# An expert stage with two units, not one, on the early routing: seven pairs and five singles follow in turn

## The chip, the core and the metric

The kernel runs on one core of a Trainium2 chip. The metric is the time of one execution on the device in microseconds, lower is better. PE is the matrix engine (TensorE), DVE is VectorE, ACT is ScalarE, POOL is GpSimd, SP is the engine whose queue issues most transfers.

## The reference

Attention over pooled queries, then a gated feed-forward block, then a mixture of eight experts of which each token takes two. All 1152 tokens (two batches of 576) go through all three. The change touches the last part alone:

```python
logits = x @ w_gate
noise_scale = np.log1p(np.exp(x @ w_noise))
noisy_logits = logits + noise_scale * noise
top2 = np.argpartition(-noisy_logits, 2, axis=1)[:, :2]
...
for e in range(E):
    for k in range(2):
        mask = top2[:, k] == e
        ...
        h = np.maximum(x[mask] @ w1[e], 0.0)
        out[mask] += top2_w[mask, k, None] * (h @ w2[e])
```

x is 1152 x 512, w1 is 8 x 512 x 1024, w2 is 8 x 1024 x 512, all float32.

## The kernel before

Every float32 product is made as three products of split operands (high and low parts), so each weight that is loaded is first split: a cast by ACT (w_hi, L993) and a subtraction by DVE (w_lo, L997).

**Blocks and units.** The tokens of each expert fill blocks of 128 slots, up to nine per expert. A unit is one set of expert weights (4 MB, eight loads of 512 KB) used on two blocks (a pair) or on one (a single). SEQ (L926) is the order of the units: the first, u0, then eight pairs and five singles in the order P S P P S P S P P S P S P. Which expert and which blocks the r-th pair or single has is computed on the chip (r_blocks, L869, and r_index, L911). Units past NPS pairs and NSS singles are guarded by the flag `more` (L1180); it is true when the routing needs more pairs or singles than these.

**Early routing.** The routing of the first 512 tokens (tiles 0 to 3) is computed during the feed-forward stage, in small steps that a hand-written plan (T_A, L1190) puts between its products. r_first (L824) counts the choices of these tokens, finds the most chosen expert (`ea`, `ef`), and marks its first block and, where there are 256 or more choices, its second (`sel0`). e_preload (L938) loads that expert's weights, e_gather0 (L958) gathers its tokens' rows. r_parity (L850) and `selx` take these blocks out of what r_blocks hands to the later units.

**The opening.** From L1333 to L1419 the order of u0 is written out by hand, since each engine works its instructions in program order: quarters of the first weight (up, L1054; each ends in an evacuation by ACT and DVE, up_evac, L1063), eight groups of the second (down, L1081), the splits of weights, and between them the routing of the other five tiles: gB is the top-2 chain and the slot assignment (with block sums on POOL at L747 and L749, which the product at L754 reads), gW the routing weights, gC the block lists (r_blocks), gH the one-hot tables, then r_table and r_index. Only behind these can the expert of u1 be read (`ti`, L903), its weights be loaded (wload, L987) and its rows be gathered (gather_x, L1005), transposed (x_trans, L1046) and used.

**The later units.** units (L1131) runs u1 to u13. A unit has eight pieces: four up, four down. Weights are split five pieces ahead; the load of a unit goes into one of two sets of buffers and is issued as the unit two before it is split. At piece 0 of unit u the result of u-1 is finished (finish, L1112): DVE scales it, adds the partial rows `pr`, and POOL scatters each block to the output in HBM (L1122). At piece 2, gather_o (L1012) fetches the partial rows of u from the output; it comes after the scatters of u-1, as both may name the same tokens. At piece 5 the next unit's rows are transposed, and the rows of the one after it gathered. Two PSUM banks hold up products (`ph`), so the fourth quarter of a pair needs the second one's bank to be evacuated; the evacuation by DVE stands behind finish of the unit before.

Of the kernel before, what the change touches and what calls it, by code (L numbers as in the profile page):

```python
# [21 lines left out]
def fused_kernel(ctx, tc, q, k, v, w_gate, w_val, w_out, rms_g,  # L22
# [539 lines left out]
    NPS, NSS = 8, 5  # L562
# [10 lines left out]
    def r_iotas():  # L573
# [35 lines left out]
        rtile("sel0", [P, 2])  # L609
# [214 lines left out]
    def r_first():  # L824
# [11 lines left out]
        dve.tensor_copy(rtile("ea", [P, 1], I32), kx[:, 0:1])  # L836
        dve.tensor_copy(rtile("ef", [P, 1]), kx[:, 0:1])
        yield
        d9, full = rtile("d9", [P, 1]), rtile("full", [P, 2])
        dve.scalar_tensor_tensor(d9, R["ef"], -float(NT), R["ip"], op0=ALU.mult, op1=ALU.add)  # L840
        dve.tensor_scalar(full[:, 0:1], k8[:, 0:1], float(2 * P * NE), None, op0=ALU.is_ge)
        yield
        sel, sx = R["sel0"], rtile("selx", [P, 1])
        dve.tensor_scalar(sel[:, 0:1], d9, 0.0, None, op0=ALU.is_equal)
        dve.tensor_scalar(sel[:, 1:2], d9, 1.0, full[:, 0:1], op0=ALU.is_equal, op1=ALU.mult)
        yield
        dve.tensor_tensor(sx, sel[:, 0:1], sel[:, 1:2], op=ALU.add)
        yield

    def r_parity():  # L850

        full, hot = R["full"], rtile("hot", [P, 1])
        dve.tensor_scalar(full[:, 1:2], full[:, 0:1], -1.0, 1.0, op0=ALU.mult, op1=ALU.add)
        dve.tensor_scalar(hot, R["er"], R["ef"], full[:, 1:2], op0=ALU.is_equal, op1=ALU.mult)
        yield
        dve.tensor_tensor(R["ev"], R["ev"], hot, op=ALU.not_equal)
        yield

    def r_index0():
        tab = rtile("tab0", [P, P])  # L860
        act.copy(tab[0:NCOL], PB["t"][0:NCOL, 0:P])
        yield 1
        pi = pst.tile([P, 512], F32, name="pi0", tag="T")
        pe.matmul(pi[:, 0:2], tab[0:NCOL], R["sel0"][0:NCOL], start=True, stop=True)
        yield 1
        dve.tensor_scalar(rtile("idx0", [P, 2], I32), pi[:, 0:2], float(BIG), None, op0=ALU.add)
        dve.tensor_scalar(rtile("gidx0", [P, 2], I32), pi[:, 0:2], float(BIG), QF - 1.0, op0=ALU.add, op1=ALU.min)
# [43 lines left out]
    def r_index(pl):  # L911
# [14 lines left out]
    SEQ = [None] + [(True, 0), (False, 0), (True, 1), (True, 2), (False, 1), (True, 3), (False, 2), (True, 4),  # L926
                    (True, 5), (False, 3), (True, 6), (False, 4), (True, 7)]
# [3 lines left out]
    def nblk(u):  # L931
        return 2 if u == 0 or SEQ[u][0] else 1

# [47 lines left out]
    def experts():  # L981
# [5 lines left out]
        def wload(u, i):  # L987
            if i == 0:
                c = ucol(u, 0)
                REG[u] = sp.value_load(R["ti"][0:1, c:c + 1], min_val=0, max_val=NE - 1)  # L990
# [13 lines left out]

        def gather_x(u):  # L1005
            XG[u] = mo.tile([P, 2, XW], F32, name="xg", tag="xg", bufs=1)
            for k in range(nblk(u)):
                c = ucol(u, k)
                pool.indirect_dma_start(out=XG[u][:, k], out_offset=None, in_=XD,
                                        in_offset=bass.IndirectOffsetOnAxis(ap=R["gidx"][:, c:c + 1], axis=0))  # L1010

        def gather_o(u):  # L1012
            PR[u] = wps[0].tile([P, 2, DM], F32, name="pr", tag="ws21", bufs=1)
            for k in range(nblk(u)):
                c = ucol(u, k)
                pool.indirect_dma_start(out=PR[u][:, k], out_offset=None, in_=out,
                                        in_offset=bass.IndirectOffsetOnAxis(ap=R["gidx"][:, c:c + 1], axis=0))
# [84 lines left out]
        def weight(u):  # L1102
# [3 lines left out]
            e = R["eb"][:, ucol(u, 0):ucol(u, 0) + 1] if u else R["ef"]  # L1106
# [5 lines left out]
        def finish(u):  # L1112
            n = nblk(u)
            yo = YO[u] = mo.tile([P, 2, DM], F32, name="yo", tag="yo", bufs=1)
            for k in range(n):
# [5 lines left out]
                sx = R["sidx"][:, ucol(u, k):ucol(u, k) + 1] if u else R["idx0"][:, k:k + 1]  # L1121
                pool.indirect_dma_start(out=out, out_offset=bass.IndirectOffsetOnAxis(ap=sx, axis=0),  # L1122
# [212 lines left out]
    gH = r_hot(4, 5, ex["mo"], (("oha", 1), ("ohs", 3)), ())  # L1335
    w_hi(0, 0)
# [7 lines left out]
    r_trans(8, (ps, "gv1", 2))  # L1344
    up(0, 0, 1)
    r_logits(7, 4, 5)
    r_logits(8, 4, 5)
    run(gB, 1)
    w_hi(0, 3)
    up_evac(0, 0)  # L1350
    ex["weight"](0)
    up(0, 1, 0)
    run(gB, 6)
    w_lo(0, 3)
    up(0, 1, 1)
# [91 lines left out]
```

## Time and profile before

| | us |
|---|---|
| three runs | 859.11, 855.58, 857.98 |
| median | 857.98 |
| the profiled execution | 858.63 |
| its span, first to last instruction | 856.8 |
| PE busy in it | 796.3 (93%) |

Lines of the profile name the engine, the line of the kernel, the operation, the tile written and the tiles read. A busy PE is not PE at its peak; PEclk is the granted clock as a share of full speed. Stages by the timeline: attention and feed-forward up to about 537, the expert stage from there to the end.

### The profile page before, as it was taken

The numbers are of one execution on the slowest core, as the hardware profiler recorded it, in microseconds if no ns is written. First come the engines' busy times: TensorE is split into PE (matmuls) and PEld (weight loads), VectorE is DVE, ScalarE is ACT, GpSimd is POOL, SyncE is SP. The second block draws the span as 40 slices with busy tenths as digits, with TensorE's granted clock in tenths as the row PEclk, the third lists the DMA queues.
The fourth block names the chain that finished last, engine by engine and source line by source line (L and its number), as shares of the span: only waits on it lengthen the run. The fifth ranks groups of instructions, "written<-read, shape, count | busy, mean of one in ns | idle before, by whom it ended". The sixth has DMA issues, their size and how long they took to land. (4 is left out here: it accounts for less than half of the span.)

```text
span 856.8 us, 14036 instructions
## 1 busy us (share of the span) xinstructions
PE 796.3 (93%) x5282; PEld 685.7 (80%) x5282; DVE 576.7 (67%) x833; ACT 421.7 (49%) x823; POOL 300.3 (35%) x251
## 2 busy tenths in 40 slices
PE   5999999999898989999999999879989998998993
PEld 4777777777675889999999899859979887998892
DVE  5667667778688755775787454767667666567670
ACT  4665565666565554442333343435635636356550
POOL 8647646649124522221222101013324133132320
PEclk9999999999998989999999999999999999999997
DMA  7344312310133112221331116069997978778410
GB/s 219 88 135 126 101 53 80 101 43 15 42 113 99 50 50 94 103 99 50 99 99 54 50 36 225 26 226 367 375 315 251 303 230 271 239 236 274 144 53 17
DMA packets 72938, 118.82 MB, mean 139 GB/s; under 512 B 7582, under 2 KB 37278, under 8 KB 72864
## 3 DMA queue, kind: packets, MB, share of 16 engines
q1 hardware_dynamic: 67504, 101.55, 37.4%
q0 software_dynamic: 5360, 16.31, 5.5%
q8 instruction: 43, 0.70, 0.4%
q14 instruction: 31, 0.25, 0.1%
HBM read 103.66 MB, written 10.77 MB: 134 GB/s over the span
## 5 line engine op out<-in xcount | busy, mean ns | idle before, releaser
L528 PE MATMUL gv<-XN,ws 128*128 128x256 f32 (+1 forms) x1152 | 168.8, 300 | 4.1 <-ACT sl L536 3.7
L528 PEld LDWEIGHTS gv<-XN,ws 128*128 128x128 f32 x1152 | 160.5, 192 | 10.1 <-ACT sl L536 4.0
L999 DVE TENSOR_TENSOR wz<-raw,wz 128x1024 fp32r<-128x1024 f32 x112 | 133.9, 1221 | 17.7 <-ACT wz L106 17.5
L193 DVE TENSOR_REDUCE Ql<-s 128x1 fp32r<-128x1152 f32 x72 | 97.3, 1355 | 59.0 <-PE s L188 45.1
L1088 PE MATMUL py<-wz,hTT 128*128 128x512 f32 x552 | 134.1, 395 | 0.0
L204 ACT ACTIVATE et<-st 128x288 f32<-128x288 f32 x288 | 103.2, 413 | 54.1 <-PE st L203 49.5
L106 ACT CAST wz<-raw 128x1024 fp32r<-128x1024 f32 x112 | 113.5, 1047 | 10.8 <-PE py L1088 8.0
L1088 PEld LDWEIGHTS py<-wz,hTT 128*128 128x128 f32 x552 | 101.4, 190 | 20.1 <-DVE hTT L971 0.9
L1061 PE MATMUL ph<-xgT,wz 128*128 128x256 f32 x768 | 97.6, 290 | 13.3 <-DVE hTT L1066 12.6
L1061 PEld LDWEIGHTS ph<-xgT,wz 128*128 128x128 f32 x768 | 96.3, 198 | 14.9 <-DVE hTT L1066 13.4
L202 PE MATMUL st<-QH,KT 128*128 128x288 f32 x288 | 91.6, 333 | 5.5 <-ACT et L204 4.0
L398 POOL TENSOR_TENSOR ws<-wm,ws 128x1024 fp32r<-128x1024 f32 x18 | 43.3, 2406 | 151.5 <-ACT ws L397 97.5
L549 PE MATMUL po<-ws,hT 128*128 128x512 f32 x324 | 83.0, 395 | 0.1
L203 PE MATMUL st<-QlT,KT 128*128 128x288 f32 x288 | 82.4, 300 | 0.0
L229 PE MATMUL av<-et,v 128*64 128x288 f32 x576 | 81.9, 420 | 0.0
L202 PEld LDWEIGHTS st<-QH,KT 128*128 128x128 f32 x288 | 55.4, 192 | 20.8 <-ACT et L204 11.6
L217 POOL TENSOR_TENSOR accp<-accp,et 128x576 f32<-128x576 f32 x32 | 48.5, 1517 | 57.1 <-ACT et L204 36.5
L549 PEld LDWEIGHTS po<-ws,hT 128*128 128x128 f32 x324 | 58.4, 188 | 10.7 <-ACT hT L538 0.5
L538 ACT CAST hT<-sl 128x256 fp32r<-128x256 f32 (+1 forms) x48 | 20.8, 434 | 89.4 <-DVE sl L537 89.4
L1122 POOL DMA_INDIRECT out_dram<-yo,sidx x21 | 27.8, 1325 | 90.4 <-DVE yo L1120 52.0
L229 PEld LDWEIGHTS av<-et,v 128*64 128x64 f32 x576 | 37.5, 138 | 26.0 <-issue 5.9
L1065 ACT ACTIVATE hTT<-ph 128x512 fp32r<-128x512 f32 x36 | 21.5, 598 | 72.7 <-PE ph L1061 70.6
(252 smaller groups left out, 1174.3 us busy)
## 6 DMA issues: line engine op xcount, KB each, us to landing
raw<-in_moe_w_dram SPq DMA_DIRECT2D x112, 512.0 KB
wraw<-in_moe_w_gate_dram SPq DMA_DIRECT2D x6, 1024.0 KB
wraw<-in_moe_w_val_dram SPq DMA_DIRECT2D x6, 1024.0 KB
wraw<-in_moe_w_out_dram SPq DMA_DIRECT2D x6, 1024.0 KB
kraw<-in_k_dram SPq DMA_DIRECT2D x16, 288.0 KB
v<-in_v_dram SPq DMA_DIRECT2D x8, 576.0 KB
KT<-KT SPq DMA_DIRECT2D x16, 288.0 KB
Qraw<-in_q_dram SPq DMA_DIRECT2D x16, 256.0 KB
```

The source lines that it names most:

```text
L106: act.copy(o, i)
L193: dve.tensor_reduce(Ql[p % 3][h][:, c, D:D + 1], t[:, :, 0:384], axis=AX.XY, op=ALU.max, negate=True)
L202: pe.matmul(t[:, 0:NG], KT[p, h][:, cs], QhT[p, h][:, n0:n0 + NG], start=True, stop=False)
L203: pe.matmul(t[:, 0:NG], KT2[h][p % NKT[h]][:, cs], QlT[p, h][:, n0:n0 + NG], start=False, stop=True)
L204: act.activation(et[:, h, :], t[:, 0:NG], AF.Exp, scale=SCALE)
L217: eng.tensor_tensor(acc, acc, e, op=ALU.add)
L229: pe.matmul(av[h * D:(h + 1) * D, 0:NG], V[p][:, h, c, :], ET[p, g, c][:, h, :], start=(c == 0), stop=(c == KC - 1))
L528: pe.matmul(t[:, 0:n], w[a][:, d, j * P:(j + 1) * P], XN[hf][b_][:, d, cs], start=(k_ == 0), stop=(k_ == 11))
L549: pe.matmul(pt, HT[f, hf][a][:, j, c0:c0 + P], w[b_][:, j, :], start=(k_ == 0), stop=(k_ == 5))
L999: eng.tensor_tensor(lo, RAW[u % 2][i], hi.bitcast(F32), op=ALU.subtract)
L1061: pe.matmul(o, w[a][:, d, j * P:j * P + P], XT[u][c][:, d], start=z + d == 0, stop=z == 2 and d == 3)
L1088: pe.matmul(PL[u, "y", k], x[c][:, f0 + d, k * P:k * P + P], w[a][:, d], start=i == 4 and z + d == 0, stop=i == 7 and z == 2 and d == 1)
```

## The change

- r_first takes the two most chosen experts of the first 512 tokens. For each, block 0 counts if it has at least 128 choices and block 1 if it has at least 256. `sel0` has four columns, and r_parity and r_index0 follow it (not shown: the parity of an expert is flipped where just one block was taken, and the index tables become four columns wide).
- u0 and u1 are both units of the early routing. u1's weights are loaded and its rows gathered (from the first 512 rows alone) at the start of the opening; u0 is as before.
- NPS is 7, not 8, and the order is now P P, then P S P S P S P S P S P P.
- The opening is written anew: ACT and DVE split weights of u0 earlier, its evacuations stand ahead of routing steps, the transposes of u1 stand between its fifth and sixth piece, and the first splits of u1 follow sooner. The gather and the loads of u2 are issued ahead of u0's last down group.

```diff
@@ -559,7 +559,7 @@
     NCOL = NE * NT
 
     NPA, NSA = 12, NE
-    NPS, NSS = 8, 5
+    NPS, NSS = 7, 5
     NCU = 2 * NPA + NSA
     BIG = B * SQ
     dram = ctx.enter_context(tc.tile_pool(name="xd", bufs=1, space=bass.MemoryType.DRAM))
...
@@ -833,27 +833,33 @@
         yield
         dve.max_index(kx, k8, key)
         yield
-        dve.tensor_copy(rtile("ea", [P, 1], I32), kx[:, 0:1])
-        dve.tensor_copy(rtile("ef", [P, 1]), kx[:, 0:1])
-        yield
-        d9, full = rtile("d9", [P, 1]), rtile("full", [P, 2])
-        dve.scalar_tensor_tensor(d9, R["ef"], -float(NT), R["ip"], op0=ALU.mult, op1=ALU.add)
-        dve.tensor_scalar(full[:, 0:1], k8[:, 0:1], float(2 * P * NE), None, op0=ALU.is_ge)
+        dve.tensor_copy(rtile("ea", [P, 2], I32), kx[:, 0:2])
+        dve.tensor_copy(rtile("ef", [P, 2]), kx[:, 0:2])
+        yield
+
+        d9, full = rtile("d9", [P, 2]), rtile("full", [P, 2, 2])
+        dve.scalar_tensor_tensor(d9, R["ef"], -float(NT), R["ip"].to_broadcast([P, 2]), op0=ALU.mult, op1=ALU.add)
+        for k in range(2):
+            dve.tensor_scalar(full[:, :, k], k8[:, 0:2], float((k + 1) * P * NE), None, op0=ALU.is_ge)
         yield
         sel, sx = R["sel0"], rtile("selx", [P, 1])
-        dve.tensor_scalar(sel[:, 0:1], d9, 0.0, None, op0=ALU.is_equal)
-        dve.tensor_scalar(sel[:, 1:2], d9, 1.0, full[:, 0:1], op0=ALU.is_equal, op1=ALU.mult)
-        yield
-        dve.tensor_tensor(sx, sel[:, 0:1], sel[:, 1:2], op=ALU.add)
+        for z in range(2):
+            for k in range(2):
+                dve.tensor_scalar(sel[:, 2 * z + k:2 * z + k + 1], d9[:, z:z + 1], float(k), full[:, z, k:k + 1],
+                                  op0=ALU.is_equal, op1=ALU.mult)
+        yield
+        dve.tensor_reduce(sx, sel, axis=AX.X, op=ALU.add)
         yield
 
     def r_parity():
 
-        full, hot = R["full"], rtile("hot", [P, 1])
-        dve.tensor_scalar(full[:, 1:2], full[:, 0:1], -1.0, 1.0, op0=ALU.mult, op1=ALU.add)
-        dve.tensor_scalar(hot, R["er"], R["ef"], full[:, 1:2], op0=ALU.is_equal, op1=ALU.mult)
-        yield
-        dve.tensor_tensor(R["ev"], R["ev"], hot, op=ALU.not_equal)
+        full, hot, odd = R["full"], rtile("hot", [P, 2]), rtile("odd", [P, 2])
+        dve.tensor_tensor(odd, full[:, :, 0], full[:, :, 1], op=ALU.subtract)
+        for z in range(2):
+            dve.tensor_scalar(hot[:, z:z + 1], R["er"], R["ef"][:, z:z + 1], odd[:, z:z + 1], op0=ALU.is_equal, op1=ALU.mult)
+        yield
+        for z in range(2):
+            dve.tensor_tensor(R["ev"], R["ev"], hot[:, z:z + 1], op=ALU.not_equal)
         yield
 
     def r_index0():
...
@@ -923,13 +929,13 @@
 
     RAW = []
     REG = {}
-    SEQ = [None] + [(True, 0), (False, 0), (True, 1), (True, 2), (False, 1), (True, 3), (False, 2), (True, 4),
-                    (True, 5), (False, 3), (True, 6), (False, 4), (True, 7)]
+    SEQ = [None, None] + [(True, 0), (False, 0), (True, 1), (False, 1), (True, 2), (False, 2), (True, 3), (False, 3),
+                          (True, 4), (False, 4), (True, 5), (True, 6)]
     NU1 = len(SEQ)
     SEQ += [(True, r) for r in range(NPS, NPA)] + [(False, r) for r in range(NSS, NSA)]
 
     def nblk(u):
-        return 2 if u == 0 or SEQ[u][0] else 1
+        return 2 if u < 2 or SEQ[u][0] else 1
 
     def ucol(u, k):
         pair, r = SEQ[u]
...
@@ -986,8 +992,8 @@
 
         def wload(u, i):
             if i == 0:
-                c = ucol(u, 0)
-                REG[u] = sp.value_load(R["ti"][0:1, c:c + 1], min_val=0, max_val=NE - 1)
+                c = ucol(u, 0) if u > 1 else 1
+                REG[u] = sp.value_load(R["ti" if u > 1 else "ea"][0:1, c:c + 1], min_val=0, max_val=NE - 1)
             e_dma(u, i)
 
         def w_hi(u, i, eng=act):
...
@@ -1002,19 +1008,24 @@
             w_hi(u, i)
             w_lo(u, i)
 
+        def col(u, k, nm):
+            if u < 2:
+                return R[nm + "0"][:, 2 * u + k:2 * u + k + 1]
+            c = ucol(u, k)
+            return R[nm][:, c:c + 1]
+
         def gather_x(u):
             XG[u] = mo.tile([P, 2, XW], F32, name="xg", tag="xg", bufs=1)
             for k in range(nblk(u)):
-                c = ucol(u, k)
-                pool.indirect_dma_start(out=XG[u][:, k], out_offset=None, in_=XD,
-                                        in_offset=bass.IndirectOffsetOnAxis(ap=R["gidx"][:, c:c + 1], axis=0))
+                gi = col(u, k, "gidx")
+                pool.indirect_dma_start(out=XG[u][:, k], out_offset=None, in_=XD if u > 1 else XD[0:QF],
+                                        in_offset=bass.IndirectOffsetOnAxis(ap=gi, axis=0))
 
         def gather_o(u):
             PR[u] = wps[0].tile([P, 2, DM], F32, name="pr", tag="ws21", bufs=1)
             for k in range(nblk(u)):
-                c = ucol(u, k)
                 pool.indirect_dma_start(out=PR[u][:, k], out_offset=None, in_=out,
-                                        in_offset=bass.IndirectOffsetOnAxis(ap=R["gidx"][:, c:c + 1], axis=0))
+                                        in_offset=bass.IndirectOffsetOnAxis(ap=col(u, k, "gidx"), axis=0))
 
         tb = [0]
 
...
@@ -1333,6 +1343,9 @@
     gW = r_weights(4, 5)
     gC = r_blocks()
     gH = r_hot(4, 5, ex["mo"], (("oha", 1), ("ohs", 3)), ())
+    ex["gather_x"](1)
+    for i in range(8):
+        wload(1, i)
     w_hi(0, 0)
     w_lo(0, 0)
     w_hi(0, 1)
...
@@ -1342,78 +1355,72 @@
     up(0, 0, 0)
     w_lo(0, 2)
     r_trans(8, (ps, "gv1", 2))
+    w_hi(0, 3)
+    w_lo(0, 3)
     up(0, 0, 1)
     r_logits(7, 4, 5)
     r_logits(8, 4, 5)
+    up_evac(0, 0)
     run(gB, 1)
-    w_hi(0, 3)
-    up_evac(0, 0)
+    up(0, 1, 0)
+    w_hi(0, 4)
     ex["weight"](0)
-    up(0, 1, 0)
     run(gB, 6)
-    w_lo(0, 3)
+    w_lo(0, 4)
     up(0, 1, 1)
+    up_evac(0, 1)
+    w_hi(0, 5)
+    up(0, 2, 0)
     run(gB, 6)
-    up_evac(0, 1)
-    w_hi(0, 4)
-    up(0, 2, 0)
-    run(gB, 11)
-    w_lo(0, 4)
+    w_lo(0, 5)
     up(0, 2, 1)
     up_evac(0, 2)
-    w_hi(0, 5)
+    run(gB, 11)
+    w_hi(0, 6)
     up(0, 3, 0)
     run(gB, 2)
-    w_hi(0, 6)
+    w_lo(0, 6)
     up(0, 3, 1)
     run(gB, 1)
-    w_lo(0, 5)
     up_evac(0, 3)
-    run(gW, 4)
     down(0, 4, 0)
     run(gB)
+    w_hi(0, 7)
+    down(0, 4, 1)
+    run(gW)
     run(gC, 2)
-    down(0, 4, 1)
+    x_trans(1)
+    down(0, 5, 0)
     run(gH, 1)
-    run(gC, 4)
-    w_lo(0, 6)
-    w_hi(0, 7)
-    down(0, 5, 0)
     run(gC, 2)
-    run(gW)
+    w_lo(0, 7)
+    down(0, 5, 1)
+    run(gC, 2)
     run(gH, 1)
     run(gH, 1)
     run(gH)
-    down(0, 5, 1)
+    w_hi(1, 0)
+    down(0, 6, 0)
     run(gC, 2)
-    wload(1, 0)
-    wload(1, 1)
-    wload(1, 2)
-    wload(1, 3)
+    w_lo(1, 0)
     r_table(4, 5)
-    r_index(ex["mo"])
-    ex["gather_x"](1)
-    w_lo(0, 7)
-    down(0, 6, 0)
     down(0, 6, 1)
     run(gC)
-    for i in range(4, 8):
-        wload(1, i)
-    w_hi(1, 0)
-    w_lo(1, 0)
-    down(0, 7, 0)
-    down(0, 7, 1)
-    w_hi(1, 1)
-    w_lo(1, 1)
-    ex["finish"](0)
-    x_trans(1)
+    r_index(ex["mo"])
     ex["weight"](1)
     ex["gather_x"](2)
-    ex["gather_o"](1)
-    for i in range(2, 5):
-        wsplit(1, i)
     for i in range(8):
         wload(2, i)
+    w_hi(1, 1)
+    down(0, 7, 0)
+    w_lo(1, 1)
+    down(0, 7, 1)
+    w_hi(1, 2)
+    w_lo(1, 2)
+    ex["finish"](0)
+    ex["gather_o"](1)
+    for i in range(3, 5):
+        wsplit(1, i)
     for i in range(5):
         wload(3, i)
     fps.close()
```

## Rows read from the trace of the kernel before

**Rows 1.** The page's costliest groups: busy us, mean ns | idle before.
```profile
L1088 PE MATMUL py<-wz,hTT 128*128 128x512 f32 x552 | 134.1, 395 | 0.0
```

**Rows 2.** Windows: busy us (x count) by engine, PEclk, DMA share, GB/s.
```profile
536.70:576.20 39.50, 31.22 (x204) 26.88 (x204) 27.76 (x86) 15.30 (x28) 5.11 (x7) 0.95 0.34 115
576.20:599.90 23.70, 23.69 (x148) 21.72 (x149) 17.95 (x24) 13.56 (x17) 6.86 (x6) 0.94 1.07 370
599.90:842.20 242.30, 229.58 (x1481) 208.25 (x1479) 160.29 (x201) 124.03 (x157) 70.31 (x56) 0.98 0.73 238
```

**Rows 3.** Waits of PE, 536.7 to 576.2: us, times, longest.
```profile
PE xt L966 <- DMA xg<-XD,gidx: 3.4, 2, 3.0
PE ph L1061 <- DVE hTT L1066: 1.9, 1, 1.9
PE pq L889 <- DVE u L885: 1.6, 1, 1.6
```

**Rows 4.** Timeline of PE: start, us, operation, count [idle before <- releaser].
```profile
550.50 1.89 PE L1061 MATMUL ph<-xt,wz 128*128 128x256 f32 x12 [1.93 <-DVE hTT L1066]
...
552.38 2.91 PE L1061 MATMUL ph<-xt,wz 128*128 128x256 f32 x12
...
576.21 12.48 PE L1061 MATMUL ph<-xgT,wz 128*128 128x256 f32 x96 [0.68 <-ACT xgT L969]
...
639.32 11.47 PE L1061 MATMUL ph<-xgT,wz 128*128 128x256 f32 x96
```

**Rows 5.** Windows right behind a wait of PE.
```profile
550.50:555.30 4.80, 4.80 (x29) 4.71 (x30) 4.66 (x23) 2.57 (x4) 0.99 (x1) 0.64 0.01 2
...
576.20:580.20 4.00, 3.99 (x23) 3.99 (x24) 3.97 (x7) 2.79 (x3) 0.99 (x1) 0.64 1.05 382
...
624.70:627.70 3.00, 3.00 (x25) 3.00 (x26) 2.78 (x3) 0.00 (x0) 0.21 (x1) 1.00 1.08 361
```

**Rows 6.** Timeline of DVE in the opening.
```profile
537.33 3.49 DVE L999 TENSOR_TENSOR wz<-raw,wz 128x1024 fp32r<-128x1024 f32 x3
...
554.02 0.20 DVE L736 TENSOR_TENSOR mmb<-M 128x40 bf16<-128x40 f32 x1
...
562.38 1.62 DVE L798 TENSOR_TENSOR ohs<-i,cs 128x512 fp32r<-128x512 f32 x3
```

**Rows 7.** Timeline of POOL: the block sums.
```profile
554.31 1.11 POOL L747 TENSOR_TENSOR sm<-mmb 128x8 bf16<-128x8 bf16 x1 [25.24 <-DVE mmb L736]
...
556.05 0.31 POOL L749 TENSOR_TENSOR mx<-sm,mmb 128x72 bf16<-128x72 bf16 x1
```

**Rows 8.** Waits of PE, 599.9 to 842.2.
```profile
PE ph L1061 <- DVE hTT L1066: 12.6, 4, 3.5
```

**Rows 9.** Timeline of PE: pairs behind a single.
```profile
687.12 4.53 PE L1061 MATMUL ph<-xgT,wz 128*128 128x256 f32 x24 [3.50 <-DVE hTT L1066]
...
791.17 4.36 PE L1061 MATMUL ph<-xgT,wz 128*128 128x256 f32 x24 [2.79 <-DVE hTT L1066]
```

**Rows 10.** Timeline of POOL: scatters of yo, gathers of pr.
```profile
692.78 0.95 POOL L1016 DMA_INDIRECT pr<-out_dram,gidx  x1 [0.31 <-issue]
...
703.97 1.03 POOL L1122 DMA_INDIRECT out_dram<-yo,sidx  x1 [0.30 <-issue]
...
717.64 1.05 POOL L1016 DMA_INDIRECT pr<-out_dram,gidx  x1 [4.70 <-DMA out_dram<-yo,sidx]
...
807.76 1.02 POOL L1122 DMA_INDIRECT out_dram<-yo,sidx  x1 [0.30 <-issue]
...
815.45 1.27 POOL L1016 DMA_INDIRECT pr<-out_dram,gidx  x1 [2.01 <-DMA out_dram<-yo,sidx]
```

**Rows 11.** Timeline of DVE: a pair's result, a single's result.
```profile
702.76 1.40 DVE L1120 SCALAR_TENSOR_TENSOR yo<-py,wv,pr 128x512 f32<-128x512 f32 x2
...
725.25 0.75 DVE L1120 SCALAR_TENSOR_TENSOR yo<-py,wv,pr 128x512 f32<-128x512 f32 x1 [4.95 <-DMA pr<-out_dram,gidx]
```

**Rows 12.** The tile pr: its gathers.
```profile
DMA to landing us min/median/max: 4.0/6.0/7.5
```

More of the change, by code (lines that the diff above doesn't have):

```diff
@@ L608, in r_iotas @@
         rtile("sel", [P, NCU])
-        rtile("sel0", [P, 2])
+        rtile("sel0", [P, 4])
     def r_consts():
@@ L863, in r_index0 @@
         pi = pst.tile([P, 512], F32, name="pi0", tag="T")
-        pe.matmul(pi[:, 0:2], tab[0:NCOL], R["sel0"][0:NCOL], start=True, stop=True)
+        pe.matmul(pi[:, 0:4], tab[0:NCOL], R["sel0"][0:NCOL], start=True, stop=True)
         yield 1
-        dve.tensor_scalar(rtile("idx0", [P, 2], I32), pi[:, 0:2], float(BIG), None, op0=ALU.add)
-        dve.tensor_scalar(rtile("gidx0", [P, 2], I32), pi[:, 0:2], float(BIG), QF - 1.0, op0=ALU.add, op1=ALU.min)
+        dve.tensor_scalar(rtile("sidx0", [P, 4], I32), pi[:, 0:4], float(BIG), None, op0=ALU.add)
+        dve.tensor_scalar(rtile("gidx0", [P, 4], I32), pi[:, 0:4], float(BIG), QF - 1.0, op0=ALU.add, op1=ALU.min)
     def r_blocks():
@@ L1105, in weight @@
             wv = WV[u] = mo.tile([P, 3, 2], F32, name="wv", tag="wv", bufs=3)
-            e = R["eb"][:, ucol(u, 0):ucol(u, 0) + 1] if u else R["ef"]
+            e = R["eb"][:, ucol(u, 0):ucol(u, 0) + 1] if u > 1 else R["ef"][:, u:u + 1]
             for z in range(2):
@@ L1120, in finish @@
                     dve.scalar_tensor_tensor(yo[:, k], PL[u, "y", k], w, PR[u][:, k], op0=ALU.mult, op1=ALU.add)
-                sx = R["sidx"][:, ucol(u, k):ucol(u, k) + 1] if u else R["idx0"][:, k:k + 1]
-                pool.indirect_dma_start(out=out, out_offset=bass.IndirectOffsetOnAxis(ap=sx, axis=0),
+                pool.indirect_dma_start(out=out, out_offset=bass.IndirectOffsetOnAxis(ap=col(u, k, "sidx"), axis=0),
                                         in_=yo[:, k], in_offset=None, bounds_check=B * SQ - 1, oob_is_err=False)
```

## The prediction, on record before the change was run

> **What bounds the kernel now.** I name the units of the expert stage by their place in SEQ: u0 is the unit that already uses the early routing, u1 the next, u13 the last; a pair works on two blocks of 128 tokens, a single on one.
>
> I first asked the page for the amount of work. The down products come 552 times [rows 1]; a pair has 48 of them and a single 24, so 552 = 9 x 48 + 5 x 24: nine pairs and five singles ran, and the guarded rest behind `more` did not. After the change it is again nine pairs (two early, seven later) and five singles. So TensorE's work is the same, and only its waits and its clock can change.
>
> Next I cut the expert stage into three stretches [rows 2]. From 536.7 to 576.2 us, the opening, u0 runs beside the routing of the other tokens, and TensorE is busy 31.22 of 39.5 us: 8.28 us of waits. From 576.2 to 599.9, u1, it never waits. From 599.9 to 842.2 it is busy 229.58 of 242.3: 12.7 us of waits. Everything ahead of 536.7 is the same program but for a few VectorE instructions.
>
> The waits of the opening are three [rows 3]: 3.4 us for the gathered rows of u1, 1.9 for an evacuation behind the routing chain in VectorE's queue, 1.6 for the block list. Behind two of them the granted clock is mostly at the lower of its two levels, 1.2 GHz (0.64 over these 4 to 5 us) [rows 5], and this costs time: 96 up products take 11.47 us at full clock, so 12 take 1.43, but after the wait at 550.5 two twelves take 1.89 and 2.91, 1.94 too much, and u1's 96 take 12.48, 1.0 too much [rows 4]. All that better cover could give back is therefore 8.28 + 1.94 + 1.0 = 11.2 us.
>
> **The change, part by part.** *Does the split fit?* Worked out from the reference on its inputs, the first 512 tokens choose experts 6 and 3 most, 457 and 357 times. Both reach 256, so both early pairs have two full blocks. The remaining blocks are exactly 7 pairs and 5 singles, so `more` stays false.
>
> *Early routing.* Five more tiny VectorE instructions, at 0.20 us each like the one at 554.02 [rows 6], beside a TensorE that is the bound there: 0 to 1.0 us, taken 0.2, because only a few of them stand ahead of something TensorE waits for.
>
> *u1's rows and weights early.* gather_x(1) moves from behind the index of all tokens to about 537, and the eight loads of u1 move to the same place on SP's queue, behind the store of the last activations. There the DMA engines are nearly idle (share 0.34 over the whole opening, 1.07 during u1 [rows 2]), so 4 MB lands long before TensorE is through u0. The 3.4 us wait goes. POOL has nothing behind the gather until the block sums at 554.3, so nothing is held up by it. SP next issues the small weight stores, which are not ready until some 15 us later.
>
> *What is late next: the routing chain on VectorE.* Each weight split costs 3.49 / 3 = 1.16 us [rows 6]. In the new order the evacuation of the second quarter stands ahead of the second batch of the routing chain, so the 1.9 us wait goes. But two more splits stand ahead of the mask `mmb`. Ahead of it from 537.3 on: 7 splits (8.1), 3 evacuations of 512 columns (half a split, 0.6 each: 1.8), 3 small ones for the weights of u0 (0.6), about 23 of the routing chain (4.6), and about 1.0 of waiting for ScalarE: 553.4, where it was at 554.02. POOL then needs from 554.31 to 556.36, 2.05 us, for the block sums [rows 7], so they are there at 555.5. TensorE, without the old waits and slow clock, finishes the first down group at about 553.05 and the next two tiny products at 553.3: it waits 2.2 us, where before a down group covered this. Its second down group and u1's transposes then run to 558.3. Behind these VectorE has two subtractions of 512 columns (1.2), the first one-hot table (half the others, 0.8), the block list (0.6), one split (1.16), the selection (0.8) and the one-hots (1.62 [rows 6]): 558.4 + 6.2 = 564.6. TensorE, with its next three down groups through at about 563, meets this chain with some 1.6 us of waits in sum (0.15 for the block list, 0.3 for its selection, the rest for the one-hots). With 0.3 for the first split, as before, new waits are 4.1 us. The work without the slow clock is 31.22 - 1.94 = 29.3. A slow clock behind the 2.2 us wait costs 0 to 1.9; I take 0.9, since waits of this stage were followed by it in some cases and not in others [rows 5]. u1 then starts at 536.7 + 29.3 + 4.1 + 0.9 = 571.0 instead of 576.2: **-5.2**, and its own slow clock goes: **-1.0**. Bounds: nothing waits, 566.0 (-10.2); the chain holds TensorE until u1 starts where it did (0). The evacuation of u0's result, 1.4 us, now borders u1's first bank; it lies inside these bounds.
>
> *The next loads.* Those of u2 hang on the block list `ti`, done at about 565.0, and u2 starts at about 593: 4 MB at the 370 GB/s of u1's stretch [rows 2] is 11.3 us, so they are in time. The gather of u2 is released by the same chain.
>
> *The order of pairs and singles.* All waits of the last stretch are one pattern: 12.6 us in four waits of TensorE for an hTT evacuation [rows 8], each in a pair that follows a single. The chain behind it: POOL scatters the pair's rows (703.97, and again when that has landed), then gathers the single's partial rows (717.64) [rows 10]; the single's result needs them, arrives at VectorE at 725.25 after 4.95 us of waiting [rows 11], and the pair's evacuations queue behind it. Three of the four were followed by the slow clock: 24 products took 4.53 us in the first and 4.36 in the last of these, against 11.47 / 4 = 2.87, so about 1.5 more [rows 9]; the other was not (1.00 behind its wait [rows 5]). In the last single (u12) no weights were loading: scatter at 807.76, gather already at 815.45, and no wait [rows 10]. Before, pairs follow a single five times: u3, u6, u8, u11 with a wait and u13 without. After, u4, u6, u8, u10, u12. Four fall as before; I count all with the slow clock: **+1.5** (0 to 1.5). The fifth, u11 to u12, has one pair still behind it, but its last weights are issued some 7 us into the single, so only the first scatter meets full traffic: 0 to 3.2 + 1.5 = 4.7, taken 0, as nearer to the last single's row.
>
> The sum: -5.2 - 1.0 + 1.5 + 0.2 = **-4.5**. The profiled execution took 858.63 us, giving 854.1; it stands 0.65 above the median of 857.98, so the forecast is **853.5**. A measurement can tell about 0.5% from no change, here 853.7 to 862.3: the forecast lies at that edge.
>
> **The rivals.** *The opening is filled* (0.14): the new waits stay under a microsecond because VectorE, busy only 27.8 of the 39.5 us of the opening [rows 2], pulls the chain forward further than I count. u1 starts at about 567; -9.2 - 1.0 + 1.7 = -8.5: about 849.5. For it: the chain has more cover, transposes and a down group between its steps. Against: with u1's splits and transposes moved in, VectorE has nearly as much work there as TensorE.
>
> *The chain takes the place of the gather* (0.18): TensorE meets the block sums and one-hots for 8 us instead of 4, and u1 starts near 575: -1.2 - 1.0 + 1.7 = -0.5, about 857.5. For it: two more splits and u1's transposes stand in VectorE's queue there. Against: the order puts work of TensorE between the steps.
>
> *Slower* (0.07): the strict turn-taking keeps POOL's scatter and gather chain from catching up. In the single pair that stood between two singles with loads running behind it, u6, the second gather was issued at 692.78 [rows 10] and its rows wanted at 702.76 [rows 11]: with 0.95 us to issue and a median of 6.0 to land [rows 12] some 3 us of room. After the change there are four such pairs. It decides once landing takes over 9 us there; at 12 us each of the four pairs is late by 3, and the single behind it again: 8 x 3 = 24, so -4.5 + 24 = +19.5, about 877. Against it: the longest landing seen is 7.5 us [rows 12], and the DMA engines are less loaded once u1's weights are in early.
>
> *The gathers land sooner* (0.03): with 4 MB of weights out of the way, gathers land in the 4.0 us of the fastest one [rows 12], the chain behind each single ends in time as in the last one, and all four waits go, 12.6 + 4.5 for the slow clock: -5.2 - 1.0 + 0.2 - 17.1 = -23.1, about 835. Against it: DMA stays busy through the last stretch (share 0.73 [rows 2]), and under that the waits arose. The Trainium skill (DMA: Bandwidth & Descriptors, section "Anatomy of one DMA — SWDGE (gpsimd) path") has a rule that goes this way: a fixed 2.0 us and bytes over 436e3 per us, for a gather of 264 KB an estimate of 2.6 us; the trace of before, with a median of 6.0, does not agree.
>
> *The split does not fit* (0.01): seven pairs or five singles overflow, the rest runs, and over 100 us are added. The counts above speak against it.
>
> **How the numbers follow.** The forecast's own case (0.57) spans about 850.5 to 856.5 and splits 0.36 faster, 0.21 same. With the filled opening and the sooner gathers, faster is 0.53; with the chain, same is 0.39; slower is 0.07 + 0.01 = 0.08. The range runs from the opening filled without any wait (858.0 - 11.2 = 846.8) to the chain holding all it gave, the extra slow clock and part of the fifth wait (859.5): 847.0 to 859.5.
>
> **What would show it.** Right: u1's first up product near 571; a new wait of about 2 us of TensorE at the block sums; no wait for xg; u1's products at full clock; four waits behind singles of about 3.2 us, none or little in u12. Wrong: u1 starting at 567 or at 575; a fifth full wait; gathers landing later than 9 us.

## The result and the profile after

| | before | after | ratio (95% interval) |
|---|---|---|---|
| median, us | 858.38 | 849.81 | 0.9894 (0.986 to 0.9927) |
| lowest to highest, us | 855.58 to 859.11 | 845.21 to 851.83 | |
| the profiled execution, us | 858.63 | 845.21 | |
| its span, us | 856.8 | 843.3 | |

The change makes the kernel faster: by 1.1% going by the ratio, by 8.6 us between the medians (a ratio here can differ a little from the quotient of the medians). The forecast was 4.5 us. The execution that was profiled is the shortest one, 4.6 us below its median, so its trace is to be read with care: a second trace of the same kernel stands below.

The work is the same: again nine pairs and five singles. From the page of the changed kernel, the group that answers to [rows 1]:

```profile
L1099 PE MATMUL py<-wz,hTT 128*128 128x512 f32 x552 | 134.2, 395 | 0.0
```

The three stretches of the expert stage, cut at the same instructions as [rows 2] (windows; busy us by engine, PEclk, DMA share, GB/s):

```profile
536.80:569.91 33.11, 29.44 (x206) 25.53 (x204) 29.13 (x90) 16.47 (x29) 3.04 (x6) 1.00 0.56 179
569.91:593.33 23.42, 23.42 (x152) 21.46 (x153) 16.74 (x20) 10.99 (x14) 6.71 (x6) 1.00 1.06 371
593.33:828.69 235.36, 227.34 (x1477) 205.79 (x1475) 159.85 (x200) 123.80 (x156) 70.21 (x55) 0.99 0.73 237
```

The opening lasts 33.11 us instead of 39.5, at full clock all through (1.00, was 0.95), and DMA is busier in it (0.56, was 0.34). u1 is 0.3 us shorter. The last stretch is 6.9 us shorter, which was in no term of the prediction's sum. The waits of TensorE from 515 us on (us, times, longest), against [rows 3, 8]:

```profile
PE ph L1072 <- DVE hTT L1077: 7.7, 3, 3.2
PE ph L1072 <- DVE yo L1129: 0.9, 1, 0.9
PE pn L754 <- POOL mx L749: 0.9, 1, 0.9
PE xt L972 <- DMA xg<-XD,gidx: 0.8, 1, 0.8
PE pp L738 <- DVE mmb L736: 0.5, 1, 0.5
PE ph L1072 <- DVE wz L1005: 0.5, 1, 0.5
PE tab L821 <- DVE ohs L798: 0.4, 2, 0.2
PE pv L904 <- DVE sel L900: 0.3, 1, 0.3
PE ph L1072 <- issue: 0.3, 1, 0.3
```

The 3.4 us for u1's rows are gone (the 0.8 for xg is u0's gather, at 530.7), and so is the evacuation behind the routing chain. In their place stand small waits on that chain: the mask, the block sums, the selection, the one-hots, and a new one of 0.9 us for `yo`. Where the chain stands, from the timelines of DVE and of POOL, against [rows 6, 7]:

```profile
553.61 0.19 DVE L736 TENSOR_TENSOR mmb<-M 128x40 bf16<-128x40 f32 x1
```

```profile
553.89 0.19 POOL L747 TENSOR_TENSOR sm<-mmb 128x8 bf16<-128x8 bf16 x1 [23.53 <-DVE mmb L736]
...
554.71 0.31 POOL L749 TENSOR_TENSOR mx<-sm,mmb 128x72 bf16<-128x72 bf16 x1
```

The mask comes at 553.6 (forecast 553.4). From POOL's first sum to its last the sums take 1.1 us, not 2.05, as the first of them took 0.19 us instead of 1.11 (the last section says what goes with that). The products that answer to [rows 4, 9], from the timeline of TensorE:

```profile
569.91 11.78 PE L1072 MATMUL ph<-xgT,wz 128*128 128x256 f32 x96 [0.93 <-DVE yo L1129]
...
593.33 11.56 PE L1072 MATMUL ph<-xgT,wz 128*128 128x256 f32 x96
...
641.03 4.62 PE L1072 MATMUL ph<-xgT,wz 128*128 128x256 f32 x24 [3.21 <-DVE hTT L1077]
...
678.94 3.08 PE L1072 MATMUL ph<-xgT,wz 128*128 128x256 f32 x24 [0.28 <-issue]
...
717.88 3.08 PE L1072 MATMUL ph<-xgT,wz 128*128 128x256 f32 x24 [2.91 <-DVE hTT L1077]
...
755.54 3.08 PE L1072 MATMUL ph<-xgT,wz 128*128 128x256 f32 x24 [1.62 <-DVE hTT L1077]
```

u1 starts at 569.9. Behind singles there are still four waits, at u4, u6, u8 and u10, and none at u12, but in this execution they are 3.2, 0.3, 2.9 and 1.6 us (the one of 0.3 has no releaser in the trace), and only one is followed by slow products (4.62 us for 24).

So three questions: is the shorter last stretch the change's doing, and if so, by its order of units or by its early loads; which of the two early things, rows or weights, gives the opening; and what are the waits behind singles worth.

### The profile page after: what moved, and what is told of

Its sections match the earlier page's. It is cut to its first block, busy times and chain, and to the rows that moved or that the text cites. A ratio compares the mean times of both kernels' runs of the same rounds, so it can differ in the third digit from the quotient of the medians.

```text
span 843.3 us, 14036 instructions
## 1 busy us (share of the span) xinstructions
PE 791.6 (94%) x5282; PEld 681.8 (81%) x5282; DVE 580.2 (69%) x838; ACT 421.4 (50%) x823; POOL 299.7 (36%) x251
## 4 chain that ended last, share of the span: by engine, by line
PE 67%; DVE 12%; issue 7%; DMA 4%; ACT 4%; POOL 4%; POOLq 0%; DVEq 0%; ACTq 0%
PE gv L528 14%; PE py L1099 11%; PE ph L1072 8%; PE po L549 8%; PE av L229 7%; PE st L202 4%; PE s L188 3%; DMA pr<-out_dram,gidx 3%; PE st L203 3%; PE ph L1087 3%; PE tt L135 2%; DVE wz L1005 2%; DVE Ql L193 1%; PE xt L972 1%; DVE es L217 1%
## 5 line engine op out<-in xcount | busy, mean ns | idle before, releaser
L1072 PE MATMUL ph<-xgT,wz 128*128 128x256 f32 x768 | 95.3, 285 | 9.0 <-DVE hTT L1077 7.7
L1072 PEld LDWEIGHTS ph<-xgT,wz 128*128 128x128 f32 x768 | 94.1, 191 | 10.8 <-DVE hTT L1077 8.4
```

Of the source, the lines that this page charges most:

```text
L1072: pe.matmul(o, w[a][:, d, j * P:j * P + P], XT[u][c][:, d], start=z + d == 0, stop=z == 2 and d == 3)
```

## The experiments

All times are medians in us; each kernel was run in turn with the kernel before on the same chip, and the ratio is to that. after_again, order_old, before_new_order and late_loads ran on one chip, late_loads2, late_gather, sums_covered and finish_late on a second, before_finish_late, order_old_finish_late and both on a third, bank_free on a fourth. The kernel before had medians of 858.75, 857.70, 858.99 and 860.74 there, so a difference of one microsecond between medians of two chips shows nothing by itself.

| run | median | ratio | 95% interval |
|---|---|---|---|
| after_again | 850.97 | 0.992 | 0.9889 to 0.995 |
| order_old | 852.66 | 0.994 | 0.991 to 0.9971 |
| before_new_order | 859.74 | 1.0023 | 0.9995 to 1.005 |
| late_loads | 859.63 | 1.002 | 0.9991 to 1.0049 |
| late_loads2 | 861.74 | 1.0038 | 1.0009 to 1.0066 |
| late_gather | 857.46 | 0.999 | 0.9958 to 1.0021 |
| sums_covered | 850.68 | 0.9913 | 0.9884 to 0.9943 |
| finish_late | 834.36 | 0.9725 | 0.9693 to 0.9758 |
| before_finish_late | 842.49 | 0.9815 | 0.9791 to 0.9838 |
| order_old_finish_late | 835.01 | 0.9726 | 0.9703 to 0.9749 |
| both | 833.34 | 0.9711 | 0.9687 to 0.9735 |
| bank_free | 832.06 | 0.9668 | 0.9641 to 0.9696 |

### after_again: the changed kernel unaltered

> The changed kernel once more, unaltered. Its first profile has 8.0 us of TensorE waits behind singles in the last stretch, against 12.6 before, and slow products behind one of them only. If this is the mechanism of the change, a second profile shows 7 to 9 us again and the median is near 850; if it was the luck of one execution, the waits are back at about 12 us and the median is nearer to 852 to 853.

850.97, with executions from 846.15 to 855.13. The one profiled now is among the longest, 855.12. The last stretch of it (windows), and TensorE's waits in it (timeline):

```profile
593.64:837.90 244.26, 231.25 (x1477) 209.82 (x1475) 159.88 (x201) 123.76 (x156) 69.47 (x55) 0.97 0.71 228
```

```profile
642.17 5.49 PE L1072 MATMUL ph<-xgT,wz 128*128 128x256 f32 x24 [4.05 <-DVE hTT L1077]
...
684.07 4.62 PE L1072 MATMUL ph<-xgT,wz 128*128 128x256 f32 x24 [3.41 <-DVE hTT L1077]
...
723.99 3.09 PE L1072 MATMUL ph<-xgT,wz 128*128 128x256 f32 x24 [2.32 <-DVE hTT L1077]
...
763.14 4.62 PE L1072 MATMUL ph<-xgT,wz 128*128 128x256 f32 x24 [3.17 <-DVE hTT L1077]
```

Opening and u1 are the same in the two traces (u2 starts at 593.64, there at 593.33). The last stretch takes 244.26 here and 235.36 there: 8.9 of the 9.9 us between the two executions. The waits are 12.9 and 8.0 us, three and one of them followed by slow products. The shorter last stretch of the first trace was that execution's, not the change's. The median of 850.97 does not decide between the two expectations (850, or 852 to 853); the two traces do.

Behind TensorE's waits stands VectorE, which waits for the single's partial rows (after_again, from 590 us on: us, times, longest):

```profile
DVE yo L1131 <- DMA pr<-out_dram,gidx: 20.3, 5, 5.8
```

The gathers of these rows took, in the first trace of the changed kernel and then in this one:

```profile
DMA to landing us min/median/max: 4.1/5.2/6.2
```

```profile
DMA to landing us min/median/max: 3.4/4.3/7.4
```

The trace with the sooner median has the longer waits, 12.9 us against 8.0. What sets their size in an execution stays open.

### order_old and before_new_order: the order of units alone

```diff
-    SEQ = [None, None] + [(True, 0), (False, 0), (True, 1), (False, 1), (True, 2), (False, 2), (True, 3), (False, 3),
-                          (True, 4), (False, 4), (True, 5), (True, 6)]
+    SEQ = [None, None] + [(False, 0), (True, 0), (True, 1), (False, 1), (True, 2), (False, 2), (True, 3), (True, 4),
+                          (False, 3), (True, 5), (False, 4), (True, 6)]
```

> The changed kernel with the kinds of units in the order of before (P P S P P S P S P P S P S P); the early routing of two units and the new opening stay. Theory A, that the new order of units shortens the waits behind singles: the last stretch is back at about 12.6 us of waits and three slow stretches, only the opening's 6.6 us stay, about 852 (0.992). Theory B, that the early loads of u1 relieve the DMA queues and so the waits: they stay near 8 us, and the time equals that of the changed kernel within 1.5 us. The prediction's own count (order costs 1.5): 848.

852.66. Its waits behind singles in its profiled execution:

```profile
PE ph L1072 <- DVE hTT L1077: 10.3, 4, 3.6
```

10.3 us lie between the two traces of the changed kernel (8.0 and 12.9). One of the four shows that the length of a wait does not settle what follows it: 3.62 us, and the 24 products behind it at full clock.

```profile
617.83 3.14 PE L1072 MATMUL ph<-xgT,wz 128*128 128x256 f32 x24 [3.62 <-DVE hTT L1077]
```

The mirror image is the kernel before with P P P S P S P S P S P S P P:

> The kernel before with its units in the order P P P S P S P S P S P S P P; one unit on the early routing, the old opening. Theory A (the order gives the gain of the last stretch): waits behind singles fall to about 8 us, 853 to 854 (0.994). Theory B (the early loads give it): waits stay at about 12.6 us, no change, 857 to 859. The prediction's own count: 1.5 us slower, 860.

859.74. The new order costs 1.0 us in the old opening and gives 1.7 in the new one, in both cases with overlapping intervals: no difference that these executions can tell. order_old alone came where theory A put it (about 852), but the theory wanted 853 to 854 for before_new_order, with the order as the one thing changed, and that came at 859.74. Theory A falls.

### late_loads and late_loads2: u1's weights as late as before

```diff
     ex["gather_x"](1)
-    for i in range(8):
-        wload(1, i)
...
-    w_hi(1, 0)
     down(0, 6, 0)
     run(gC, 2)
+    sp.value_load(R["ti"][0:1, 0:1], min_val=0, max_val=NE - 1)
+    for i in range(8):
+        wload(1, i)
+    w_hi(1, 0)
     w_lo(1, 0)
     r_table(4, 5)
```

> The changed kernel, but the weights of u1 are loaded only once the block list is known (SP waits for ti first), where the kernel before loads them; rows of u1 are still gathered early. Theory B (early loads relieve the queues): DMA runs at its full share from 565 to about 635 again, the waits behind singles go back to about 12 us, and the time is 4 to 7 us above the changed kernel. Theory A (order): the waits stay near 8 us, and only u1's first splits come later, 0 to 2 us.

859.63, 8.7 above the changed kernel on the same chip and more than either theory said: the whole gain is lost. But not by the way of theory B: the waits behind singles are 6.7 us in its profile, and 3.1 more inside a single, no more than in the changed kernel. Most of the loss is in the opening, on ACT and TensorE (timelines):

```profile
570.24 1.04 ACT L106 CAST wz<-raw 128x1024 fp32r<-128x1024 f32 x1 [7.55 <-DMA raw<-in_moe_w_dram]
```

```profile
571.50 0.64 PE L922 MATMUL pi<-sel,tabs 72*128 72x32 f32 x2 [4.54 <-ACT tabs L919]
...
577.64 11.78 PE L1072 MATMUL ph<-xgT,wz 128*128 128x256 f32 x96 [1.40 <-DVE yo L1129]
```

ACT stood 7.55 us before the cast of a weight that had not landed, and the copy of the index table, behind it in its order, came too late: u1 at 577.6 instead of 569.9, of which 1.0 us is a later start of the whole opening in this execution. Counted from the transposes of the eighth tile (537.83 here, 536.80 there) the opening takes 39.81 us instead of 33.11, which is 6.7 of the 8.7. late_loads2 takes that cast out of the way, to behind the copy (shown against late_loads):

```diff
-    w_hi(1, 0)
-    w_lo(1, 0)
     r_table(4, 5)
...
-    w_hi(1, 1)
+    w_hi(1, 0)
     down(0, 7, 0)
+    w_lo(1, 0)
+    w_hi(1, 1)
     w_lo(1, 1)
     down(0, 7, 1)
```

> As late_loads, but ACT's first cast of u1's weights stands behind the copy of the index table, so that a late weight can no longer hold up the index. Theory C (the 8.7 us that late_loads lost were a wait that ACT passed on: its cast of u1's first weights stood ahead of the index copy, 4.5 us of TensorE waiting there and u1 at 577.6): u1 now starts at 570 to 572 and the time is within 2.5 us of the changed kernel (850 to 853). Rival D (u1's loads at 565 are too late for it in any order, since 4 MB in the queue also holds up the gathers): u1's up products wait for weights, or u2 is late, and 5 us or more of the loss stay (856 or more).

861.74: theory C falls as it was put, and the time is in the range of rival D. On TensorE, and on DVE:

```profile
576.78 14.15 PE L1072 MATMUL ph<-xgT,wz 128*128 128x256 f32 x96 [8.16 <-DVE yo L1129]
```

```profile
569.93 1.23 DVE L1005 TENSOR_TENSOR wz<-raw,wz 128x1024 fp32r<-128x1024 f32 x1 [3.37 <-ACT wz L106]
...
574.75 1.22 DVE L1005 TENSOR_TENSOR wz<-raw,wz 128x1024 fp32r<-128x1024 f32 x1 [1.46 <-ACT wz L106]
575.89 1.40 DVE L1129 TENSOR_SCALAR yo<-py,wv 128x512 f32<-128x512 f32 x2
```

The wait has moved to `yo`, u0's result. DVE makes it behind three splits of u1, which now wait for weights that land from 568.9 on, and u1's first bank waits for it (bank_free shows this link by itself). So the new opening, in the two orders tried, needs the early weights: without them each place where a split stands ahead of something else hands the wait on. An order with late weights in which nothing stands behind the splits was not tried, so rival D, that they are too late in any order, stays open. In part the trace bears it out: the first split of u1, which its first products read, ends at 571.2, 34.7 us after the eighth tile's transposes (536.46), where the changed kernel starts u1 33.1 us after them. By these rows an estimate of 1.6 us of the loss is the weights' own.

### late_gather: u1's rows as late as before, its weights early

```diff
-    ex["gather_x"](1)
     for i in range(8):
         wload(1, i)
...
-    x_trans(1)
...
     r_index(ex["mo"])
-    ex["weight"](1)
-    ex["gather_x"](2)
+    pool.tensor_tensor(rtile("hold", [P, 5]), R["eb"][:, 0:5], mhalf, op=ALU.mult)
+    ex["gather_x"](1)
...
     ex["finish"](0)
+    x_trans(1)
+    ex["weight"](1)
+    ex["gather_x"](2)
     ex["gather_o"](1)
```

> The changed kernel with its early loads, but u1's rows are gathered only when the block list is known (POOL waits for it), and transposed behind u0's last piece, as in the kernel before. The prediction's step (the gathered rows are the wait that the change removes): TensorE waits 3 us or more for xg again, u1 starts at 573 to 576, and the time is 3 to 6 us above the changed kernel, 854 to 857. Rival: with no weights in the queues the gather lands in under 5 us, so that the last down group covers most of it: u1 starts at 571 to 572 and at most 2 us are lost.

857.46, just past the far end of the first expectation (854 to 857). TensorE at the start of u1:

```profile
569.13 1.12 PE L972 MATMUL xt<-ident,xg 128*128 128x128 f32 x4 [2.23 <-DMA xg<-XD,gidx]
...
572.26 1.11 PE L972 MATMUL xt<-ident,xg 128*128 128x128 f32 x4 [2.02 <-DMA xg<-XD,gidx]
...
574.05 13.96 PE L1072 MATMUL ph<-xgT,wz 128*128 128x256 f32 x96 [0.68 <-ACT xgT L975]
```

The waits for xg are back (4.2 us), u1 starts at 574.05, 4.1 later, and its up products take 13.96 us instead of 11.78. These two make 6.3 of the 6.5 to 7.7 us lost against the two medians of the changed kernel. The rival (a gather in an idle queue is covered) falls. Both early things are needed, and in the orders tried each alone is worth nothing.

### finish_late: a single's result finished later

In `units`, the result of a single is finished behind the pair's third up piece, not its first, and thus behind two evacuations of the pair in DVE's order:

```diff
-                if i == 0 and u > max(u0, 1):
+                if i == (2 if nblk(u - 1) == 1 else 0) and u > max(u0, 1):
                     finish(u - 1)
```

> The changed kernel, but in a pair behind a single the single's result is finished after the third up piece, not the first, so that the pair's first evacuations no longer queue on DVE behind the gathered partial rows. Theory E (the waits behind singles are DVE's queue order, and they are what makes two executions of one kernel differ by up to 10 us): the 8 to 13 us of these waits and the slow clock behind them go, the time falls by 8 to 14 us to 836 to 843, and the executions lie closer together, within 5 us. Rival: the late result makes the next scatter and gather late in turn, and the waits come back one unit later: 848 or more.

834.36, all six executions between 833.52 and 834.67, and lower than expected (836 to 843). The opening, u1, and from u2 to the last product (windows):

```profile
535.92:568.84 32.92, 29.51 (x205) 25.60 (x205) 29.16 (x90) 17.80 (x30) 3.04 (x6) 1.00 0.55 181
568.84:592.26 23.42, 23.42 (x152) 21.45 (x153) 16.74 (x20) 10.99 (x14) 6.70 (x6) 1.00 1.06 371
592.26:817.00 224.74, 224.74 (x1477) 204.18 (x1475) 160.93 (x200) 123.80 (x156) 68.92 (x55) 1.00 0.76 248
```

TensorE does not wait once in the last 224.74 us, at full clock, and VectorE's wait for the partial rows is gone from its trace. Theory E holds, and its rival falls: the later result makes nothing late that TensorE would wait for. The waits behind singles cost about 16 us by the medians. In the two traces of the changed kernel the last stretch is 10.6 and 19.5 us longer than here, 8.0 and 13.0 of it waits and 2.6 and 6.5 more time of busy products: the expectation had put too little on the slow clock. The executions lie within 1.2 us here, where they lay 9 us apart in after_again, so these waits are what spread them; the next run shows the same of the kernel before (2.5 us apart).

### before_finish_late and order_old_finish_late: the change without those waits

The same edit in the kernel before, and in order_old.

> The kernel before, with the late finish behind singles. If the waits behind singles are the same in both kernels and the change's gain is the opening and u1 alone (u1 6.3 us earlier, u2 6.6 to 7.7), this kernel loses its 17 us (12.6 of waits and 4.6 of slow clock) to 840 to 843, and stands 6 to 8 us above the changed kernel with the late finish (834.4). If part of the change's gain was in the last stretch, the two stand closer than 6 us or, the other way, 10 us apart or more.

> The changed kernel in the old order of units, with the late finish. With the waits behind singles gone, the order should cost nothing: within 1 us of 834.4. If strict turn-taking itself costs or gains something (weights late, POOL's queue), they differ by 2 us or more.

842.49 and 835.01. With the spread gone, the change is worth 842.49 - 834.36 = 8.1 us. finish_late ran on another chip; on one chip the change in the old order of units is worth 842.49 - 835.01 = 7.5. The new order gains 0.65 of the 8.1, if that difference between two chips is real. TensorE of before_finish_late at u1 and u2, and its opening, u1 and last stretch (windows):

```profile
574.64 13.99 PE L1061 MATMUL ph<-xgT,wz 128*128 128x256 f32 x96 [0.68 <-ACT xgT L969]
...
599.85 4.40 PE L1076 MATMUL ph<-wz,xgT 128*128 128x256 f32 x36
```

```profile
535.19:574.64 39.45, 31.27 (x205) 26.89 (x205) 27.76 (x86) 15.30 (x28) 5.10 (x7) 0.95 0.35 120
574.64:599.85 25.21, 25.21 (x148) 23.23 (x149) 17.94 (x24) 13.55 (x17) 7.51 (x6) 0.88 1.07 371
599.85:824.00 224.15, 224.15 (x1481) 203.83 (x1479) 161.57 (x200) 123.97 (x157) 70.91 (x56) 1.00 0.77 253
```

The opening there starts at 535.19 (the transposes of the eighth tile) and in finish_late at 535.92, u1 at 574.64 and 568.84, u2 at 599.85 and 592.26. So the opening takes 39.45 and 32.92, u1 25.21 and 23.42: 6.5 + 1.8 = 8.3 us. Behind u2 the two take 224.15 and 224.74 us, neither with a wait. The gain of the change is its opening and the clock of u1 (0.88 there, 1.00 here), and nothing from u2 on.

### sums_covered, both and bank_free: what is left in the opening

```diff
+    down(0, 4, 1)
     run(gB)
     w_hi(0, 7)
-    down(0, 4, 1)
     run(gW)
```

> The changed kernel with the second down group of u0's first piece ahead of the block sums instead of behind them, as in the kernel before. The wait of 1.5 us at mmb and mx goes; what it held back (block list, one-hots) comes 1.4 us of TensorE work later only where TensorE was early. If VectorE's chain sets u1's start, nothing is gained (same within 1 us); if TensorE's waits add up, as the prediction's sum has it, u1 starts 1 to 1.5 us earlier, 848 to 850.

850.68, where 848 to 850 was expected if the microsecond came through. The opening is shorter: the wait for the block sums is 0.24 us, and u1 starts 1.08 us sooner when both are counted from the wait for the first split (537.23 and 538.88 in the two traces).

```profile
553.41 0.19 PE L754 MATMUL pn<-onesb,mx 128*72 128x2 bf16 x1 [0.24 <-POOL mx L749]
...
567.18 11.78 PE L1072 MATMUL ph<-xgT,wz 128*128 128x256 f32 x96 [0.94 <-DVE yo L1129]
```

The time can't show a microsecond while executions differ by seven; with the late finish it can:

> The changed kernel with the late finish and the second down group ahead of the block sums. sums_covered brought u1 1.06 us forward, which its own time could not show among executions that lie 7 us apart. With the late finish they lie 1 us apart: 833.0 to 833.6 if the microsecond is kept to the end, 834.4 if it is given back.

833.34, 1.0 below finish_late. That is a difference between two chips; what shows the microsecond is the traces, u1 31.87 us after the eighth tile's transposes instead of 32.92. The last run moves u0's result ahead of a split:

```diff
+    ex["finish"](0)
     w_hi(1, 2)
     w_lo(1, 2)
-    ex["finish"](0)
```

> The kernel of the run both, with u0's result finished ahead of the third split of u1 on DVE, not behind it. In every kernel of the new opening u1's first product waits 0.9 us for yo. If that is u1's first bank being one of those that hold u0's result, the wait goes (the result is read out 1.15 us sooner) and the time falls by 0.9 us, to 832.2 to 832.8. If the wait is only put down to yo and is something else, u1 starts where it did and the time stays at 833.3.

832.06. The wait for `yo` is gone:

```profile
567.26 11.74 PE L1072 MATMUL ph<-xgT,wz 128*128 128x256 f32 x96
```

From the transposes of the eighth tile (536.47 here, 535.60 in both) u1 starts after 30.79 us instead of 31.87. So the wait was u1's first bank, held by u0's result. This kernel is 3.3% below the kernel before.

## Why the prediction came out as it did, point by point

**The split fits.** Right: 552 down products, and no rest.

**u1's rows.** Right, in place and kind: the early gather takes away the 3.4 us wait, and late_gather brings it back.

**u1's weights.** Right that they are hidden, but priced at nothing in themselves. They are a condition of the new order: it puts splits of u1 ahead of the index copy and of u0's result, and late weights make the opening 6.7 and 7.2 us longer there (late_loads, late_loads2). The prediction asked what stands behind a moved gather, not what stands behind a moved split.

**What is late next.** Right in kind and nearly in place: the mask was forecast at 553.4 and came at 553.6; the waits for mask and sums at 2.2 and came at 1.5, as POOL's sums took 1.1 us and not the 2.05 of the old trace; those for block list, selection and one-hots at 1.6, and came at 0.7. Not priced, only bounded, was the bank of u1, 0.9. In sum 33.11 - 29.44 = 3.7 us of waits against 4.1. The slow clock behind them, taken at 0.9, did not come: 1.00 through the opening. u1 started at 569.9, not 571.0, and the opening gave 6.4 to 6.5, not 5.2.

**u1's slow clock.** Right in kind; its size is one execution's. The term was -1.0, from 96 products in 12.48 us. In that trace u1 in all took 0.3 us longer than in the changed kernel. In before_finish_late, with the same opening, the 96 products took 13.99, and u1 in all 1.8 us longer than in finish_late.

**The order.** The step that failed, and the largest miss of the sum: +1.5, from counting which waits are followed by the slow clock. Its count of waits was right (four, and none at u12), but their size and what follows them are the execution's (8.0 us with one slow stretch, 12.9 with three). In place of a loss of 1.5 the runs show none: without the waits the new order is 0.65 us faster, across two chips, and with them no difference could be told.

**The instructions added.** +0.2 was taken. The opening starts from 535.2 to 536.7 us in the three traces of the old opening and from 535.3 to 537.8 in the eleven of the new, so no run can show this term.

The sum with the terms of the two kernels with the late finish, -6.5 - 1.8 + 0 = -8.3, agrees with the 8.1 between their medians (with the 0.6 us that the changed one takes longer from u2 on it is -7.7). The changed kernel itself was 8.6 us faster in the result and 7.8 in after_again. The forecast of -4.5 had the mechanism of the opening and about half of the size. The rival of the filled opening had the time (849.5), but not the way: it wanted u1 at 567, where the changed kernel does not have it; sums_covered, both and bank_free do.

**The other rivals.** No sign of POOL falling behind: the longest landing of partial rows is 6.2 and 7.4 us in the two traces of the changed kernel, under the 9 that this rival needed, and with the late finish the strict order leaves TensorE no wait in the last stretch. The gathers did not land in 4.0 us throughout either (medians of 5.2 and 4.3), and the waits stayed. finish_late comes near that rival's time (835), but by another way.

## What to carry to other kernels

A moved load or gather is worth the wait that it ends, and it holds only together with all else that the new order relies on: rows and weights early gave 8 us, either alone nothing in the orders tried. Where one instruction on an in-order engine waits for a far transfer, look at what is queued behind it; here one line that lets two evacuations pass a result gave twice what the change did. When executions of a kernel scatter by more than the effect that is sought, first find the wait that scatters, and measure with it gone.

## What the runs showed of the hardware that was not expected

- The price of TensorE's lower clock level varied from execution to execution for like waits: u1's 96 up products behind the wait for xg took 12.48 us in one execution of the old opening, 13.99 in another and 13.96 in late_gather, against 11.47 to 11.78 at full clock. Between the two of the old opening lie 1.5 us.
- A wait of 2.9 us at u8 in the first trace of the changed kernel was followed by full clock (24 products in 3.08 us), one of 3.2 us at u4 was not (4.62 us). One of 3.62 us in order_old was (3.14 us).
- A tiny POOL sum took 1.11 us in the trace of before [rows 7] and 0.19 in that of after. That is no accident of one execution: it took 1.11 in all three traces of the old opening and 0.19 or 0.20 in all eleven of the new one. Nor is it the idle time ahead of it: the same sum for the first tiles took 0.20 us behind 30.10 us of idle time, in the trace of before:

```profile
505.77 0.20 POOL L747 TENSOR_TENSOR sm<-mmb 128x8 bf16<-128x8 bf16 x1 [30.10 <-DVE mmb L736]
```

  What goes with it is VectorE. In the old opening a weight split follows the mask there, from 554.14 to 555.36, and the sum ends at 555.42. In the new opening an evacuation and small instructions follow it. That the split beside it held the sum up fits all fourteen traces, but no run moved the split alone, so it is argued and not shown:

```profile
554.14 1.22 DVE L999 TENSOR_TENSOR wz<-raw,wz 128x1024 fp32r<-128x1024 f32 x1
```
